# Sorting only the first 192 tokens' keys in the head, and moving the other keys, the later scores and the second query transpose into the first dense layer

## The chip, the cores and the metric

One core of a Trainium2 chip. The time is device time in microseconds (us), the median over executions. Engines: TensorE (PE, with its weight loads PEld), VectorE (DVE), ScalarE (ACT), GpSimd (POOL), SyncE (SP). The granted clock is the share of TensorE's full clock in the profile's records: at half clock it is 0.5. PSUM is the memory that takes the results of matmuls here; VectorE and ScalarE copy them out of it.

## The reference, cut to what matters

```python
# P: (batch 4, heads 8, 8, 8), five rounds of exp and row/column normalisation (Sinkhorn)
k_sorted = einsum('bhij,bhjcd->bhicd', P, k_blocks)   # 8 blocks of 96 rows, head_dim 64
v_sorted = einsum('bhij,bhjcd->bhicd', P, v_blocks)
scores = q_blocks @ k_sorted_blocks.T / 8             # inside each block of 96
attn   = softmax(scores) @ v_sorted_blocks
x      = attn, tokens x 512
out    = (s * relu(x @ w_in)**2 + b) @ w_out          # 512 -> 2048 -> 512
```

The sort mixes whole blocks, so one destination block of keys needs all eight source blocks, but only its own row of P. The tokens go through in 8 tiles of 384: tile 0 is destination blocks 0 to 3 of batch 0, tile 1 blocks 4 to 7. The 192 tokens of the title are blocks 0 and 1.

## The kernel before: the parts that matter here

The head, from the finished P to the first dense matmul:

```python
    k_piece(0, 0, 16, 1, "v")()     # 16 matmuls of 64 columns, copies by VectorE ("v")
    k_piece(0, 32, 16, 1, "s")()    # by ScalarE ("s")
    k_piece(0, 64, 8, 1, "v")()
    k_piece(0, 80, 8, 1, "s")()
    v_piece0(0, 16, "v")            # values: 16 matmuls and one copy
    v_piece0(16, 16, "s")
    v_piece0(32, 16, "v")
    s_piece(0, 0)                   # scores and exp of tile 0, head pair 0, four blocks
    s_piece(0, 1)
    v_piece0(48, 16, "v")
    s_piece(0, 2)
    s_piece(0, 3)
    q_half(1, "s")                  # transpose q for tile 1
    for hp in range(NHP):
        p_piece(0, hp, 0, 2)        # attn x values, blocks 0 and 1
    t_piece(0, "v", 0, 2)           # transpose them: 192 columns for the dense layer
    s_piece(1, 0)
    s_piece(1, 1)
```

Tile 0's first dense layer runs in two halves of 192 columns. Each half has eight groups, and after each group a slot for one piece of other work:

```python
    ffn1(0, Queue([P(0, 0, 2, 2), P(0, 1, 2, 2), P(0, 2, 2, 2), P(0, 3, 2, 2), SC(1, 2),
                   lambda: t_piece(0, "v", 2, 2), SC(1, 3), P(1, 0)], 8), 0, 2)
    ffn1(0, Queue([nothing, P(1, 1), nothing, P(1, 2), nothing, P(1, 3), nothing,
                   lambda: t_piece(1, "v")], 8), 2, 2)

    # in ffn1, for each group:
            hps = psa.tile([128, 2, 512], FP, tag="a", name="hps")   # one of 3 large PSUM buffers
            # ... 8 matmuls
            nc.scalar.activation(out=rt[...], in_=hps[...], func=AF.Relu)
            nc.vector.tensor_tensor(out=gt[...], in0=rt[...], in1=rt[...], op=ALU.mult)
            slot()
```

A piece in a slot is therefore issued to ScalarE and VectorE between the relu and square of one group and those of the next. The kernel's PSUM is divided into three large buffers (`psa`) and two small ones (`psb`).

The softmax here doesn't subtract the row's maximum and nothing guards it: scores larger than these inputs give would overflow.

## Time and profile before

| | before |
|---|---|
| time, median of the first 4 runs | 249.91 us (249.04 to 252.37) |
| span of the profiled run, mean granted clock | 247.8 us, 0.959 |
| first dense matmul (the head ends) | 31.04 us |
| half 1 of tile 0's first dense layer | 8.75 us |
| half 2 with its tail, up to tile 1's dense layer | 9.60 us |
| from tile 1's dense layer to the end | 198.4 us |

The last four rows come from the timeline: the starts of the 1st, 65th and 129th matmul of the dense layer's group, and the end of the span. They add up to the span, so a change can be booked row by row. The lines of the profile are shown in the prediction.

### The profile page before, as it was taken

What the parts mean: (1) busy time and instruction counts of PE and PEld (TensorE: products, weight loads), DVE (VectorE), ACT (ScalarE), POOL (GpSimd) and SP (SyncE); (2) the same over time, 40 slices, a digit from 0 to 9 for tenths busy, and PEclk for the clock granted to TensorE, in tenths of its full rate; (3) what the DMA queues carried; (4) which work ended last, traced back from release to release, by engine and by line L of the source; (5) the groups of instructions that cost most, each with busy time, mean ns of one, the idle gap of its engine ahead of it and who ended that gap; (6) DMA issues with size and microseconds to landing.
All of it is one profiled execution on the core that took longest, in us unless ns stands there. A gap on an engine that the chain in (4) does not pass through costs nothing.

```text
span 247.8 us, 4978 instructions
## 1 busy us (share of the span) xinstructions
PE 233.1 (94%) x2128; PEld 140.9 (57%) x2128; DVE 133.2 (54%) x260; ACT 116.3 (47%) x156; POOL 39.3 (16%) x51
## 2 busy tenths in 40 slices
PE   8879799799999899998899999999999999999993
PEld 4578699645554456655555555666555566664441
DVE  5776556899992545846675345444353444442221
ACT  6346566335358274477852342666341536661000
POOL 7720200497910027000000000000000000000000
PEclk9955579999999999999999999999999999999999
DMA  5999999999799929991001212000012120001122
GB/s 65 195 194 212 212 205 205 218 204 236 144 99 152 343 90 145 132 173 22 0 4 42 87 43 84 4 0 0 4 42 87 42 87 0 3 0 42 51 76 86
DMA packets 20214, 24.97 MB, mean 101 GB/s; under 512 B 7520, under 2 KB 14432, under 8 KB 19680
## 3 DMA queue, kind: packets, MB, share of 16 engines
q0 software_dynamic: 8400, 15.21, 35.8%
q1 hardware_dynamic: 11792, 9.45, 14.8%
q8 instruction: 16, 0.26, 0.5%
q14 instruction: 6, 0.05, 0.1%
HBM read 29.63 MB, written 8.65 MB: 155 GB/s over the span
## 4 chain that ended last, share of the span: by engine, by line
PE 69%; DVE 12%; DMA 9%; ACT 6%; issue 1%; SPq 0%; DVEq 0%
PE ops L459 29%; PE hps L433 27%; DMA vs<-dv 5%; PE pv L386 4%; DVE gt L438 3%; DMA dv<-vn 3%; ACT rt L437 3%; PE sc L359 3%; PE tr L414 2%; ACT ks L230 2%; PE tv L304 2%; DVE ks L228 2%; DVE qt L228 1%; PE tk L278 1%; DMA sn<-in_sort_net_dram 1%
## 5 line engine op out<-in xcount | busy, mean ns | idle before, releaser
L433 PE MATMUL hps<-xt,wi 128*128 128x384 bf16 (+1 forms) x576 | 89.2, 311 | 2.4 <-ACT ks L230 1.1
L459 PE MATMUL ops<-wo,gt 128*128 128x512 bf16 x384 | 90.5, 380 | 0.0
L433 PEld LDWEIGHTS <-wi 128*128 128x128 bf16 x576 | 54.3, 99 | 31.7 <-issue 4.1
L437 ACT ACTIVATE rt<-hps 128x768 bf16<-128x768 f32 (+1 forms) x72 | 53.2, 739 | 38.1 <-PE hps L433 34.1
L438 DVE TENSOR_TENSOR gt<-rt 128x768 bf16<-128x768 bf16 (+1 forms) x72 | 43.0, 601 | 43.2 <-ACT rt L437 42.8
L459 PEld LDWEIGHTS <-gt 128*128 128x128 bf16 x384 | 35.1, 98 | 38.4 <-issue 0.6
L450 DVE SCALAR_TENSOR_TENSOR ot<-ops,s_bc,bias 128x512 f32<-128x512 f32 x24 | 18.0, 748 | 36.4 <-PE ops L459 36.4
L362 ACT ACTIVATE at<-sc 96x768 bf16<-96x768 f32 x32 | 24.2, 802 | 24.1 <-PE sc L359 24.1
L391 DVE TENSOR_TENSOR x<-pv,rec 96x512 bf16<-96x512 f32 (+1 forms) x36 | 22.6, 628 | 1.3
L230 ACT COPY xt<-tr 128x1536 bf16<-128x1536 bf16 x6 | 8.6, 1438 | 23.6 <-PE tr L414 23.6
L228 DVE CAST ks<-tk 64x512 bf16<-64x512 f32 (+1 forms) x28 | 18.5, 662 | 1.7 <-PE tk L278 1.3
L583 POOL TENSOR_TENSOR csum<-csum,wo 128x512 f32<-128x512 f32 x14 | 17.6, 1255 | 1.0
L230 ACT CAST ks<-tk 64x512 bf16<-64x512 f32 (+1 forms) x24 | 13.9, 580 | 7.2 <-PE tk L278 6.9
L390 DVE RECIPROCAL rec<-pv 96x8 f32<-96x8 f32 (+1 forms) x36 | 7.0, 193 | 17.4 <-PE pv L386 17.4
L386 PEld LDWEIGHTS <-at 96*128 96x128 bf16 (+1 forms) x256 | 11.9, 104 | 5.6 <-DMA vs<-dv 1.5
L386 PE MATMUL pv<-vs,at 96*128 96x66 bf16 (+1 forms) x256 | 12.9, 199 | 1.8 <-DMA vs<-dv 1.0
L359 PEld LDWEIGHTS <-ks 64*96 64x96 bf16 x256 | 8.5, 132 | 6.1 <-issue 5.0
L359 PE MATMUL sc<-qt,ks 64*96 64x96 bf16 x256 | 10.8, 223 | 0.3 <-DVE ks L228 0.2
L172 PE MATMUL wp<-zt 128*128 128x256 bf16 x50 | 9.6, 321 | 1.1 <-DVE warm L104 1.1
L278 PE MATMUL tk<-pd,kb 64*128 64x64 bf16 (+1 forms) x144 | 8.3, 216 | 0.9 <-DVE pd L511 0.9
L278 PEld LDWEIGHTS <-kb 64*128 64x128 bf16 (+1 forms) x144 | 7.4, 106 | 3.0 <-issue 2.2
L228 DVE COPY qt<-tq 128x1536 bf16<-128x1536 bf16 x4 | 7.0, 1754 | 3.5 <-PE tq L259 3.5
(67 smaller groups left out, 116.8 us busy)
## 6 DMA issues: line engine op xcount, KB each, us to landing
out_dram<-ot SPq DMA_DIRECT2D x24, 256.0 KB, 2.0
kb<-in_k_dram POOLq DMA_DIRECT2D x4, 768.0 KB, 21.8
vb<-in_v_dram POOLq DMA_DIRECT2D x4, 768.0 KB, 19.0
qr<-in_q_dram POOLq DMA_DIRECT2D x3, 768.0 KB, 35.4
wi<-in_moe_w_in_dram POOLq DMA_DIRECT2D x2, 1024.0 KB, 19.1
wo<-in_moe_w_out_dram POOLq DMA_DIRECT2D x2, 1024.0 KB, 30.2
dv<-vn SPq DMA_DIRECT2D x6, 256.0 KB, 3.6
vs<-dv POOLq DMA_DIRECT2D x4, 384.0 KB, 11.3
```

What stands on the lines that cost most here:

```text
L228: nc.vector.tensor_copy(out=out, in_=in_)
L230: nc.scalar.copy(out=out, in_=in_)
L278: nc.tensor.matmul(out=ps[:, c, :], lhsT=kb[pr, c0 + 2 * c:c0 + 2 * c + 2, :].rearrange("p c d -> p (c d)"), rhs=rhs, start=True, stop=True)
L359: nc.tensor.matmul(out=sc[:, e, n * BLK:(n + 1) * BLK], lhsT=ks[pr, g0 + n, :], rhs=QT[b][pr, hp, q0:q0 + BLK], start=True, stop=True)
L362: nc.scalar.activation(out=at, in_=sc[:, :, 0:TG], func=AF.Exp, scale=scale)
L386: nc.tensor.matmul(out=pv[e][0:m, (n - n0) * VW:(n - n0 + 1) * VW], lhsT=atf[:, c0:c0 + m], rhs=VS[b][:, gi, :], start=True, stop=True)
L391: nc.vector.tensor_tensor(out=x[:, n0:n0 + nn, hp * 128:(hp + 1) * 128].rearrange("p n (e d) -> p e n d", e=2), in0=pvv[:, :, :, 0:D], in1 ...
L433: nc.tensor.matmul(out=hps[:, f, 0:nt], lhsT=wi_at(hp, f0 + f), rhs=xt[:, hp, c0:c0 + nt], start=(hp == 0), stop=(hp == NHP - 1))
L437: nc.scalar.activation(out=rt[:, :, 0:nt], in_=hps[:, :, 0:nt], func=AF.Relu)
L438: nc.vector.tensor_tensor(out=gt[:, f0:f0 + 2, c0:c0 + nt], in0=rt[:, :, 0:nt], in1=rt[:, :, 0:nt], op=ALU.mult)
L450: nc.vector.scalar_tensor_tensor(out=ot, in0=ops, scalar=s_bc, in1=bias, op0=ALU.mult, op1=ALU.add)
L459: nc.tensor.matmul(out=ops, lhsT=gt[:, f, m * 128:(m + 1) * 128], rhs=wo_at(f), start=(f == 0), stop=(f == NF - 1))
```

## The change

Its intent is to reach the first dense matmul sooner. Only what blocks 0 and 1 need is done in the head; the rest goes into slots, where TensorE was busy with dense groups anyway. The core of the diff:

```diff
-    k_piece(0, 0, 16, 1, "v")()  ... (four pieces, all 8 destination blocks)
+    k_piece0(0, 24, 0, 2, "v")      # destination blocks 0 and 1 alone: 16 columns
+    k_piece0(48, 24, 0, 2, "s")
     v_piece0(0, 16, "v")
     v_piece0(16, 16, "s")
+    s_half(0, 0, 0)                 # scores of two blocks
     v_piece0(32, 16, "v")
-    s_piece(0, 0) ... s_piece(0, 3), q_half(1, "s")
+    s_half(0, 1, 0)
-    v_piece0(48, 16, "v")
+    v_piece0(48, 8, "v")
+    s_half(0, 2, 0)
+    v_piece0(56, 8, "s")
+    s_half(0, 3, 0)
     ... p_piece x4, t_piece
-    s_piece(1, 0)
-    s_piece(1, 1)
+    def KB(c0, eng):
+        return lambda: k_piece0(c0, 16, 2, 6, eng)     # the other 6 blocks: 48 columns
+    def SH(hp):
+        return lambda: (s_half(0, hp, 2), s_half(0, hp + 1, 2))
+    ffn1(0, Queue([KB(0, "v"), KB(32, "s"), KB(64, "v"), SH(0), SH(2),
+                   seq(P(0, 0, 2, 2), P(0, 1, 2, 2)), seq(P(0, 2, 2, 2), P(0, 3, 2, 2)),
+                   lambda: t_piece(0, "v", 2, 2)], 8), 0, 2)
+    ffn1(0, Queue([lambda: q_half(1, "s"), S2(1, 0), nothing, S2(1, 2), P2(1, 0), nothing,
+                   P2(1, 2), lambda: t_piece(1, "v")], 8), 2, 2)
```

(`k_piece0` writes its results in 4 or 8 copies, and the loads of batch 2 now stand after half 1. `seq` puts several pieces into one slot; `S2` and `P2` are the scores and the attention x values of two head pairs.) A late key piece (`KB`) takes a large PSUM buffer and is emptied by 8 copies of 64 x 192 elements.

More of the change, by code (lines that the diff above doesn't have):

```diff
@@ L295, in k_piece, with k_piece0 @@
         return lambda: half(1)
+    def k_piece0(c0, nc2, i0, ni, eng):
+        pr = slice(0, 64)
+        gw = NHP * ni
+        if nc2 * 2 * gw > 512:
+            ps = psa.tile([128, 2, 512], FP, tag="a", name="tk")
+            psh = ps[:, :, 0:nc2 * gw].rearrange("p h (c w) -> p h c w", c=nc2 // 2)
+        else:
+            ps = psb.tile([128, 512], FP, tag="b", name="tk")
+            psh = ps[:, 0:nc2 * 2 * gw].rearrange("p (h c w) -> p h c w", h=2, c=nc2 // 2)
+        rhs = pd1[pr].rearrange("p e m i -> p (e m) i")[:, :, i0:i0 + ni]
+        for c in range(nc2):
+            nc.tensor.matmul(out=psh[:, c // (nc2 // 2), c % (nc2 // 2), :],
+                             lhsT=kb[pr, c0 + 2 * c:c0 + 2 * c + 2, :].rearrange("p c d -> p (c d)"),
+                             rhs=rhs, start=True, stop=True)
+        for cp in range(2):
+            for e in range(2):
+                dst = ks[e * 64:(e + 1) * 64, 0:32, c0 + cp:c0 + 2 * nc2:2].rearrange(
+                    "p (m i) c -> p m i c", i=NB)[:, :, i0:i0 + ni, :]
+                sr = psh[cp * 64:(cp + 1) * 64]
+                if sr.shape[1] * sr.shape[2] * 2 * gw <= 512:
+                    srs = [ps[cp * 64:(cp + 1) * 64, 0:nc2 * 2 * gw].rearrange(
+                        "p (c e m i) -> p e m i c", e=2, m=NHP, i=ni)[:, e]]
+                    dsts = [dst]
+                else:
+                    srs = [sr[:, h].rearrange("p c (e m i) -> p e m i c", e=2, m=NHP)[:, e]
+                           for h in range(2)]
+                    hc = nc2 // 2
+                    dsts = [dst[:, :, :, h * hc:(h + 1) * hc] for h in range(2)]
+                for d_, s_ in zip(dsts, srs):
+                    evac(d_, s_, eng)
     def v_piece0(d0, n, eng):
@@ L363, in s_piece, with s_half @@
         AT[t, hp] = at
+    def s_half(t, hp, n0, nn=2):
+        b, half = divmod(t, 2)
+        g0 = (b % 2) * 32 + hp * NB + half * HB
+        sc = psa.tile([BLK, 2, 512], FP, tag="a", name="sc")
+        for n in range(n0, n0 + nn):
+            for e in range(2):
+                pr = slice(e * 64, (e + 1) * 64)
+                q0 = (half * HB + n) * BLK
+                nc.tensor.matmul(out=sc[:, e, (n - n0) * BLK:(n - n0 + 1) * BLK],
+                                 lhsT=ks[pr, g0 + n, :], rhs=QT[b][pr, hp, q0:q0 + BLK],
+                                 start=True, stop=True)
+        at = atp.tile([BLK, 2, nn * BLK], BF, tag="at", name="ath")
+        nc.scalar.activation(out=at, in_=sc[:, :, 0:nn * BLK], func=AF.Exp, scale=scale)
+        AT[t, hp, n0] = at
     def p_piece(t, hp, n0=0, nn=HB):
         b, half = divmod(t, 2)
-        at = AT[t, hp]
+        halved = (t, hp, n0) in AT
+        at = AT[t, hp, n0] if halved else AT[t, hp]
         if t not in X:
@@ L382, in p_piece @@
             for n in range(n0, n0 + nn):
-                c0 = (e * HB + n) * BLK
-                m = 128 if c0 + 128 <= 2 * TG else BLK
+                c0 = (e * nn + n - n0) * BLK if halved else (e * HB + n) * BLK
+                m = 128 if c0 + 128 <= at.shape[1] * at.shape[2] else BLK
                 gi = e * 32 + hp * NB + half * HB + n
@@ L531 @@
     build_pd1()
-    k_piece(0, 0, 16, 1, "v")()
-    k_piece(0, 32, 16, 1, "s")()
-    k_piece(0, 64, 8, 1, "v")()
-    k_piece(0, 80, 8, 1, "s")()
+    k_piece0(0, 24, 0, 2, "v")
+    k_piece0(48, 24, 0, 2, "s")
     v_piece0(0, 16, "v")
     v_piece0(16, 16, "s")
+    s_half(0, 0, 0)
     v_piece0(32, 16, "v")
-    s_piece(0, 0)
-    s_piece(0, 1)
-    v_piece0(48, 16, "v")
-    s_piece(0, 2)
-    s_piece(0, 3)
-    q_half(1, "s")
+    s_half(0, 1, 0)
[3 more added lines that the diff above has]
+    s_half(0, 3, 0)
     for hp in range(NHP):
@@ L547 @@
     t_piece(0, "v", 0, 2)
-    s_piece(1, 0)
-    s_piece(1, 1)
-    load_v(*brows(2))
-    load_k(*brows(2))
-    load_q(2)
     def P(t, hp, *r):
@@ L563, in V1 @@
         return lambda: v_piece1(i * 8, "v")
-    ffn1(0, Queue([P(0, 0, 2, 2), P(0, 1, 2, 2), P(0, 2, 2, 2), P(0, 3, 2, 2), SC(1, 2),
-                   lambda: t_piece(0, "v", 2, 2), SC(1, 3), P(1, 0)], 8), 0, 2)
-    ffn1(0, Queue([nothing, P(1, 1), nothing, P(1, 2), nothing, P(1, 3), nothing,
-                   lambda: t_piece(1, "v")], 8), 2, 2)
+    def KB(c0, eng):
[5 more added lines that the diff above has]
+                   lambda: t_piece(0, "v", 2, 2)], 8), 0, 2)
+    load_v(*brows(2))
+    load_k(*brows(2))
+    load_q(2)
+    ffn1(0, Queue([lambda: q_half(1, "s"), S2(1, 0), nothing, S2(1, 2), P2(1, 0), nothing,
+                   P2(1, 2), lambda: t_piece(1, "v")], 8), 2, 2)
     build_pd2()
```

## The prediction

> **What bounds the kernel now.** I read three views in this order: the page of the whole run, to see which engine sets the end; the chain that ended last, to see where that engine does not; and the timeline of the first 50 us, the only part that the change touches.
>
> From the page:
>
> ```profile
> PE 233.1 (94%) x2128; PEld 140.9 (57%) x2128; DVE 133.2 (54%) x260; ACT 116.3 (47%) x156; POOL 39.3 (16%) x51
> PEclk9955579999999999999999999999999999999999
> ```
>
> TensorE is busy 94% of the span, so from the first dense layer on the end is "start of that layer plus TensorE's work". The second line has 6.2 us per digit: TensorE ran at about half clock from roughly 12 to 34 us. From the chain that ended last, from the sorting of the first keys to the first dense matmul:
>
> ```profile
> 13.53 1.88 PE tk L278 x32
> 15.43 0.74 ACT ks L230
> ...
> 18.52 2.94 PE tv L304 x32
> ...
> 24.38 1.23 DVE vs L228
> ...
> 25.65 1.49 PE tq L244 x25
> 27.14 0.35 PE pv L386 x4
> ...
> 30.29 0.80 PE sc L359 x10
> 31.10 1.40 PE hps L433 x8
> ```
>
> The reader is to see that this head is not only TensorE: copies out of PSUM by ACT and DVE stand between the matmuls. The dense layer starts at 31.0. From the timeline:
>
> ```profile
> 14.58 4.92 DVE L228 CAST ks<-tk 64x512 bf16<-64x512 f32 x8 [1.10 <-PE tk L278]
> 15.43 4.80 ACT L230 CAST ks<-tk 64x512 bf16<-64x512 f32 x8 [3.46 <-PE tk L278]
> 16.81 4.65 PE L304 MATMUL tv<-pd,vb 64*128 64x64 bf16 x48 [0.56 <-DMA vb<-in_v_dram]
> 33.05 0.36 DVE L438 TENSOR_TENSOR gt<-rt 128x384 bf16<-128x384 bf16 x1 [2.16 <-ACT rt L437]
> 33.91 0.83 PE L433 MATMUL hps<-xt,wi 128*128 128x192 bf16 x8
> 37.55 0.49 ACT L437 ACTIVATE rt<-hps 128x384 bf16<-128x384 f32 x1
> 49.38 1.47 PE L433 MATMUL hps<-xt,wi 128*128 128x384 bf16 x8
> ```
>
> Key copies occupy both copying engines for 4.9 us, but the values land only at 16.8, and their matmuls run until 24. In the dense part, TensorE goes from piece to piece without a gap: half 1 of the first dense layer runs 31.04 to 39.78 (8.7 us), half 2 with its tail until the next dense layer starts at 49.38 (9.6 us). ACT and DVE follow TensorE there with little waiting for them. One more reading matters at the end: TensorE waited 1.03 us at 82.17 for a DMA (vs<-dv), so a little slack of the DMA queues lies there.
>
> **What the Trainium skill says.** (1) "TensorE: Matmul & The Clock Gate", section on LDWEIGHTS: the load of the stationary operand scales with its columns, whatever the contraction. So a key matmul with 128 stationary columns does not get cheap when its moving side shrinks from 64 to 16. The trace agrees as far as it goes: 48 pairs took 2.72 us, 57 ns each at half clock, and 16 took 0.57 us, 36 ns each, at full clock. (2) The same page, section "Architectural detail": ACT and DVE are strict FIFO. The trace cannot contradict it, and the whole estimate below rests on it. (3) The same page, Part 1: full clock comes after about 3.4 us of sustained activity and goes after an idle window. Here the clock fell at 13.24 and rose at 33.72, 2.7 us into the dense layer. (4) "ScalarE: Activation LUTs", section "What ACT_TABLE_LOAD costs": an ACTIVATE costs 186 ns + 0.833 ns per element. For 192 elements that is 346 ns. The trace's key copies are 740 ns at 512 and 424 at 256, a slope of 1.23 ns, steeper than the page's, but it also gives 346 at 192. DVE's were 750 and 430, so it is used for both.
>
> **The change part by part.** The head sorts keys for two of eight destination blocks only, scores two blocks only, and leaves out the transpose of the second half of q and the scores of tile 1. All of that goes into the first dense layer, and the keys of batch 0 are now multiplied twice: 48 matmuls with 16 columns, then 48 with 48.
>
> *Head.* Matmuls of keys: 48 before and after, still about 2.7 us, to 16.2. Copies: 4 of 192 elements on each engine, 4 x 0.36 = 1.4 us in place of 4.9; they end near 17.7. But the values land at 16.8 as before, and the 64 value matmuls take 97 ns each (4.65/48): 6.2 us, plus four short score pieces of 0.25: TensorE is done at 24.0. The last value copy (8 wide, ACT, about 0.5) ends near 24.5, so attention x values starts there and not at 27.1: 1.45 us because the q transpose is gone, 1.1 us from copies. From there to the dense layer it took 3.95 us (27.08 to 31.04); nothing on that path is removed. Start of dense layer: 28.45. Gain 2.6 us.
>
> *Half 1 of the dense layer, counted from its start, TensorE first at half clock.* Pieces in the built order: H0 (dense group), K0 (keys, copied by DVE), H1, K1 (copied by ACT), H2, K2 (copied by DVE), H3, scores 0 and 1, H4, scores 2 and 3, H5, two pv, H6, two pv, H7, transpose. A dense group is 1.23 at half and 0.66 at full clock; a key piece 0.9 or 0.57. Each key piece has 8 copies of 192 elements: 8 x 0.36 = 2.9 us. TensorE reaches the end of K1 at 1.23+0.9+1.23+0.9 = 4.3. ACT copies K1 from 4.5 to 7.3, and only then can do the relu of H2 (7.8), because it is FIFO. DVE must square H2 (8.15) before it may copy K2: 8.15 to 11.05. Scores 0 need every key, so TensorE waits until 11.1; in the old kernel the half was over at 8.7. After that: scores and H4 to 12.2 or 12.8, exps and relus in turn on ACT (four of 0.5 each), H5's relu done near 14.5 to 15.5, then DVE alone: square 0.36, two pv results 2 x 0.62, square, two more, square, transpose copy 0.56, that is 3.6 with latencies 4.2. Half 1 ends at 18.7 (full clock from H2) to 20.2 (half clock throughout). Against 8.74: a loss of 10.0 to 11.5.
>
> *Half 2 with its tail.* Added: the q transpose (48 matmuls, 1.3; two ACT copies of 0.75 that the scores wait for), and scores 0 and 1 of tile 1 with their exps (2 x 0.80). ACT's sum is 8 x 0.49 + 1.5 + 4 x 0.80 = 8.6. With three PSUM buffers the dense groups wait for exps: H8 0 to 0.7, transposes to 2.0, copies on ACT 2.1 to 3.6, relu 4.1, exps to 5.75, two relus to 6.75, exps to 8.35, relu 8.85; then DVE's square and two pv results (0.89 each) to 11.05, squares to 12.0, two more to 13.8, square and transpose copy to 15.35, and the next layer starts at 16.0. Against 9.6: a loss of 6.4.
>
> *Later.* The next batches' loads of keys and values wait for later matmuls, but they stand in one queue behind loads that fill it until about 48 us, so they are not late. The 1.03 us wait for the DMA disappears, since loads drain while TensorE is late: gain 1.0.
>
> Sum: -2.6 + 10.7 (middle) + 6.4 - 1.0 = +13.5. TensorE's clock may fall again in the gap of half 1 and be half in part of half 2: an estimate of +0.5 for that, from the 1.5 us that such a case costs at most over half 2. Time: 249.95 + 14 = 264.
>
> **The rivals.** *A: the gain of the head carries through.* If copies hid behind dense matmuls, the cost would be TensorE's added work alone: in the dense layer 48 key matmuls at 36 ns (1.7), transposes 1.3, scores 1.0, 4.0 in all, against a head shorter by 2.6: about 251, within 2%. For it: DVE is busy 54% and ACT 47% over the run. Against it: in half 1 DVE now has 2.9 (squares) + 5.8 (keys) + 2.5 + 0.6 = 11.8 us of work where the half took 8.7. *B: faster.* If TensorE kept full clock in the head through denser work and the dense layer ran at full clock from its start, 1.3 us more would come in, 247 to 249. Against it: between 16.7 and 20.1 TensorE was already busy without gaps and the clock stayed at half. *C: the clock falls.* Gaps of 3 us in half 1 and 60% duty in half 2 keep half clock until the next layer: 267 to 268. For it: the clock stayed low through the head, where TensorE was busy 80% with small matmuls.
>
> **Range and chances.** If a key copy took 0.25 rather than 0.36 us, half 1 would lose 2.6 less; if half 2 hid half of what I charge, 3.2 less: 258. With C, 268. I take 258 to 269 as the 8 in 10. Slower by over 2% means over 254.95, which needs 5 of the 14 us only: 0.92. Within 2%: 0.06, rival A with part of the stall. Faster: 0.02.
>
> **What would show it.** The first dense matmul near 28.5 (head right). In half 1 a gap of TensorE of about 3 us that ends with DVE's key copies, near 39.5 us from the start; 24 late key copies of near 350 ns each; the first full-width dense matmul of tile 1 (128x384) near 63 to 66 in place of 49.4; no wait for vs<-dv; a lower granted clock than 0.959. It is wrong if that first full-width group comes before 56, if the copies take under 0.25 us, or if the time after that group is shorter or longer than before by more than 2 us.

## The result, and the profile after

The changed kernel takes **260.16 us** (259.28 to 260.99, 4 runs) against 249.91: the ratio is **1.039** (95% interval 1.031 to 1.048), slower. Ratios here are the mean time of one kernel's fast runs over that of the other's of the same rounds, so not quite the ratio of the medians quoted. The profiled run of the changed kernel (260.99) was the slowest of its four, so the table's +11.5 is a little more than the 10.3 between the medians.

| stage (profiled runs) | before | after | difference | predicted |
|---|---|---|---|---|
| first dense matmul | 31.04 | 27.63 | -3.4 | -2.6 |
| half 1 | 8.75 | 19.04 | +10.3 | +10.0 to +11.5 |
| half 2 with tail | 9.60 | 14.20 | +4.6 | +6.4 |
| rest | 198.37 | 198.42 | 0.0 | -1.0 + 0.5 |
| span | 247.8 | 259.3 | +11.5 | +14 |

The page of the changed kernel, the two lines that answer to the first fence of the prediction:

```profile
PE 239.5 (92%) x2156; PEld 144.0 (56%) x2176; DVE 133.0 (51%) x272; ACT 116.1 (45%) x165; POOL 39.4 (15%) x51
PEclk9955555997999999999999999999999999999999
```

DVE and ACT are no busier than before in sum; nothing in the averages shows an engine that limits the kernel. The clock line (6.5 us per digit) has five digits at half rate where there were about three, and a 7 further on. From the timeline of the changed kernel, the head; as everywhere in this view the columns are start, busy time, engine, line, operation, operands, count and, in brackets, the idle time just before and what ended it:

```profile
13.63 1.43 PE L309 MATMUL tk<-pd,kb 64*128 64x16 bf16 x48 [1.00 <-DVE pd L560]
14.45 1.54 DVE L228 CAST ks<-tk 64x192 bf16<-64x192 f32 x4 [0.97 <-PE tk L309]
...
16.82 2.85 PE L336 MATMUL tv<-pd,vb 64*128 64x64 bf16 x30 [1.76 <-DMA vb<-in_v_dram]
...
23.74 0.65 PE L435 MATMUL pv<-vs,ath 96*128 96x66 bf16 x8 [0.48 <-ACT vs L230]
```

The reader is to see the same landing of the values as before (16.8), now with TensorE idle for 1.76 us ahead of it, and attention x values starting at 23.7, not at 27.1. Then half 1, in the same view:

```profile
27.63 1.44 PE L482 MATMUL hps<-xt,wi 128*128 128x192 bf16 x8 [0.65 <-DVE xt L228]
...
29.91 2.58 DVE L228 CAST ks<-tk 64x192 bf16<-64x192 f32 x8
...
32.00 2.39 ACT L230 CAST ks<-tk 64x192 bf16<-64x192 f32 x8 [0.26 <-PE tk L309]
...
34.41 0.49 ACT L486 ACTIVATE rt<-hps 128x384 bf16<-128x384 f32 x1
...
34.94 0.36 DVE L487 TENSOR_TENSOR gt<-rt 128x384 bf16<-128x384 bf16 x1 [2.07 <-ACT rt L486]
35.33 2.57 DVE L228 CAST ks<-tk 64x192 bf16<-64x192 f32 x8
...
37.29 0.31 PE L406 MATMUL sc<-qt,ks 64*96 64x96 bf16 x1 [1.41 <-DVE ks L228]
...
37.96 0.55 PE L406 MATMUL sc<-qt,ks 64*96 64x96 bf16 x7 [0.36 <-DVE ks L228]
```

Read it downwards as one chain. ACT copies the second key piece for 2.4 us; only then, at 34.41, does it get to a relu whose matmuls had ended at about 33.4. DVE had nothing to do for 2.07 us until that relu let it square, and only then does it copy the third key piece, whose matmuls had ended at about 34.1. The scores need that copy: TensorE waits 1.41 and 0.36 us for it, after 0.33 us for ACT before the group ahead. The last part of half 1, still in this view:

```profile
43.62 0.42 DVE L440 TENSOR_TENSOR x<-pv,rec 96x256 bf16<-96x256 f32 x1
...
44.19 0.35 PE L435 MATMUL pv<-vs,ath 96*128 96x66 bf16 x4 [0.21 <-DVE x L440]
...
46.05 0.56 DVE L228 COPY xt<-tr 128x768 bf16<-128x768 bf16 x1
...
46.67 0.83 PE L482 MATMUL hps<-xt,wi 128*128 128x192 bf16 x8 [0.65 <-DVE xt L228]
```

The four attention results of blocks 2 and 3 come in the last slots, right before half 2 needs them, so half 2 waits for DVE. Later, the pieces of tile 1's first dense groups show the clock:

```profile
60.87 2.25 PE L482 MATMUL hps<-xt,wi 128*128 128x384 bf16 x8
...
63.61 2.05 PE L482 MATMUL hps<-xt,wi 128*128 128x384 bf16 x8
...
65.93 1.47 PE L482 MATMUL hps<-xt,wi 128*128 128x384 bf16 x8
```

The same group takes 1.47 us at full clock; two groups ran at half clock because the granted clock fell at 61.4 us for 3.4 us. That is 0.78 + 0.58 = 1.4 us lost, and it hides the gain of the vanished wait for the DMA (vs<-dv, 1.03 us before, none now).

### The profile page after: what moved, and what is told of

The parts are those of the page before. It is cut to its first block, busy times and chain, and to the rows that moved or that the text cites. A ratio compares the mean times of both kernels' runs of the same rounds, so it can differ in the third digit from the quotient of the medians.

```text
span 259.3 us, 5077 instructions
## 1 busy us (share of the span) xinstructions
PE 239.5 (92%) x2156; PEld 144.0 (56%) x2176; DVE 133.0 (51%) x272; ACT 116.1 (45%) x165; POOL 39.4 (15%) x51
## 4 chain that ended last, share of the span: by engine, by line
PE 75%; DVE 10%; ACT 6%; DMA 5%; issue 2%; POOL 1%; POOLq 0%
PE ops L508 31%; PE hps L482 29%; DMA vb<-in_v_dram 5%; ACT rt L486 4%; DVE ks L228 3%; PE pv L435 3%; PE sc L391 3%; DVE gt L487 2%; PE tr L463 2%; PE tv L336 2%; ACT ks L230 2%; DVE x L440 1%; DVE qt L228 1%; PE tq L259 1%; PE tv L366 1%
## 5 line engine op out<-in xcount | busy, mean ns | idle before, releaser
L482 PE MATMUL hps<-xt,wi 128*128 128x384 bf16 (+1 forms) x576 | 94.3, 322 | 4.6 <-ACT ks L230 1.4
L508 PE MATMUL ops<-wo,gt 128*128 128x512 bf16 x364 | 87.7, 379 | 1.5 <-issue 0.5
L482 PEld LDWEIGHTS <-wi 128*128 128x128 bf16 x576 | 56.9, 103 | 36.0 <-issue 6.6
L394 ACT ACTIVATE at<-sc 96x768 bf16<-96x768 f32 x28 | 21.1, 808 | 20.0 <-PE sc L391 20.0
L228 DVE CAST ks<-tk 64x192 bf16<-64x192 f32 (+1 forms) x40 | 20.3, 524 | 1.7 <-PE tk L309 1.0
L230 ACT CAST ks<-tk 64x512 bf16<-64x512 f32 (+1 forms) x28 | 13.1, 485 | 7.0 <-PE tk L278 3.4
L435 PEld LDWEIGHTS <-at 96*128 96x128 bf16 x224 | 9.6, 102 | 3.2 <-issue 0.4
L435 PE MATMUL pv<-vs,at 96*128 96x66 bf16 x224 | 9.9, 195 | 0.3 <-ACT at L394 0.3
L391 PE MATMUL sc<-qt,ks 64*96 64x96 bf16 x224 | 8.6, 210 | 0.7 <-ACT qt L230 0.3
L463 PE MATMUL tr<-ident,x 96*128 96x96 bf16 x128 | 7.7, 211 | 0.8 <-DVE x L440 0.6
L377 POOL DMA_DIRECT2D vs<-dv x4 | 5.4, 1346 | 20.5 <-DMA dv<-vn 19.1
## 6 DMA issues: line engine op xcount, KB each, us to landing
wi<-in_moe_w_in_dram POOLq DMA_DIRECT2D x2, 1024.0 KB, 18.7
```

What stands on the lines that cost most here:

```text
L228: nc.vector.tensor_copy(out=out, in_=in_)
L230: nc.scalar.copy(out=out, in_=in_)
L391: nc.tensor.matmul(out=sc[:, e, n * BLK:(n + 1) * BLK], lhsT=ks[pr, g0 + n, :], rhs=QT[b][pr, hp, q0:q0 + BLK], start=True, stop=True)
L394: nc.scalar.activation(out=at, in_=sc[:, :, 0:TG], func=AF.Exp, scale=scale)
L435: nc.tensor.matmul(out=pv[e][0:m, (n - n0) * VW:(n - n0 + 1) * VW], lhsT=atf[:, c0:c0 + m], rhs=VS[b][:, gi, :], start=True, stop=True)
L482: nc.tensor.matmul(out=hps[:, f, 0:nt], lhsT=wi_at(hp, f0 + f), rhs=xt[:, hp, c0:c0 + nt], start=(hp == 0), stop=(hp == NHP - 1))
```

## The experiments

Theory 1, from the prediction: half 1 is set by a serial chain through the two copying engines: second key piece on ACT, relu, square, third key piece on DVE, scores. Rivals: DVE's total work; the three large PSUM buffers; TensorE's added matmuls or its half clock; the late q transpose and scores rather than the keys.

| run | time | ratio to before | first dense | half 1 | half 2 | rest |
|---|---|---|---|---|---|---|
| changed kernel | 260.16 | 1.039 | 27.6 | 19.04 | 14.20 | 198.4 |
| changed_again | 259.33 | 1.043 | 26.9 | 19.05 | 14.20 | 198.4 |
| k0_twice | 260.88 | 1.048 | 26.8 | 19.98 | 14.43 | 198.2 |
| k1_twice | 262.83 | 1.056 | 27.4 | 22.09 | 14.43 | 198.0 |
| keys_split | 261.18 | 1.050 | 27.4 | 20.22 | 14.20 | 197.0 |
| keys_small_psum | 260.50 | 1.047 | 27.4 | 20.08 | 14.20 | 197.0 |
| keys_alternate | 257.75 | 1.038 | 27.4 | 16.87 | 14.20 | 197.1 |
| keys_in_head | 253.73 | 1.022 | 28.3 | 12.44 | 14.20 | 197.1 |
| q_in_head | 259.64 | 1.043 | 27.6 | 19.05 | 12.57 | 197.1 |
| keys_and_q_in_head | 252.34 | 1.017 | 29.6 | 12.63 | 14.16 | 198.1 |
| filled | 259.15 | 1.039 | 27.4 | 18.00 | 16.37 | 197.0 |
| q_late_only | 251.04 | 1.008 | 29.0 | 12.82 | 9.58 | 197.2 |
| values_split_only | 248.56 | 1.000 | 29.5 | 9.54 | 9.59 | 197.7 |

Times are medians of the fast runs; the stages are of the one profiled run each, found as in the table above. The intervals of the ratios are 0.3 to 0.6% wide on either side (0.9% in the first row), so the stages tell more than the times. The profiled run of keys_and_q_in_head was slow; it is one of its four timed runs. One of four runs of keys_in_head and two of six of values_split_only were slow too. Times and ratios leave them out. The changed kernel was run once more, in the same rounds as keys_alternate, keys_and_q_in_head and values_split_only, for a baseline:

> The changed kernel itself, for a baseline on the same chip and in the same rounds as the next three: 260 to 261 us, 1.039 to 1.047 of the kernel before.

It agrees with the first measurement; the total came out 0.7 us under the range expected, the ratio inside it. The clock took another course than in the first profile (full from 32.9 to 36.3 us, then half until 43.2), and half 1 is the same to 0.01 us: for 2.2 of those 3.4 us TensorE waited for key copies. The first dense matmul differs by 0.7 us between the two rows, and that follows the landing of the values: in eight profiles with this same head (both of these, the two `twice`, keys_split, keys_small_psum, keys_alternate, filled) the value matmuls start at 16.0 to 16.8 us and the dense layer 10.8 to 10.9 us later. It doesn't follow the fall of the clock, which comes anywhere from 12.9 to 16.1 us there.

**k0_twice and k1_twice: which copies are on the path.** The changed kernel with every copy of one late key piece written twice: the first piece (DVE), or the second (ACT).

```diff
-                for d_, s_ in zip(dsts, srs):
-                    evac(d_, s_, eng)
+                for d_, s_ in zip(dsts, srs):
+                    for _ in range(times):
+                        evac(d_, s_, eng)
-    ffn1(0, Queue([KB(0, "v"), KB(32, "s"), ...
+    ffn1(0, Queue([KB(0, "v", 2), KB(32, "s"), ...     # k0_twice; k1_twice: KB(32, "s", 2)
```

> The changed kernel with each copy of the first late key piece (on DVE) written twice: 8 more copies of about 0.32 us, 2.6 us more work for DVE. Theory 1, a serial chain (second piece copied on ACT, then the relu, then the square, then the third piece on DVE): the first piece ends before the square that gates the third, so the time grows by only 0.5 to 0.9 us over the changed kernel's 260.2. Rival, DVE's total work in the half sets its length: plus 2.6 us.

> The changed kernel with each copy of the second late key piece (on ACT) written twice: 2.4 us more work for ACT and none for DVE. Theory 1 (the serial chain runs through this piece): plus 2.4 us, about 262.6. Rival, DVE's total work sets the half: plus 0 to 0.5 us.

From the timelines, k0_twice first, then k1_twice:

```profile
29.12 5.74 DVE L228 CAST ks<-tk 64x192 bf16<-64x192 f32 x16
```
```profile
31.82 5.50 ACT L230 CAST ks<-tk 64x192 bf16<-64x192 f32 x16 [0.26 <-PE tk L309]
...
37.87 0.36 DVE L488 TENSOR_TENSOR gt<-rt 128x384 bf16<-128x384 bf16 x1 [5.19 <-ACT rt L487]
```

The extra copies took 3.1 to 3.2 us in either run (16 in 5.74 and 5.50 us, where 8 took 2.58 and 2.39), more than the 2.4 to 2.6 expected. On ACT's second piece they cost half 1 3.05 us, all of it. On DVE's first piece they cost 0.9: the changed kernel has DVE idle for 2.07 us ahead of the square that gates the third piece, and that took up two thirds of them. The totals of the two, of the same rounds, are 260.88 and 262.83. DVE's total work as the cause is ruled out: it had its extra 3.2 us in the run whose half 1 moved by 0.9.

**keys_split: a test that tested something else.** Each key piece copied half by DVE, half by ACT:

```diff
-                    evac(d_, s_, eng)
+                    evac(d_, s_, eng if ni == 2 else "vs"[cp])
```

> The changed kernel with each late key piece copied half by DVE and half by ACT, the same 24 copies. Theory 1: the second piece no longer takes ACT for 2.4 us before a relu, and the third is copied in half the time: scores of blocks 2 and 3 start 2 to 2.5 us earlier, time near 257.9. Rival, TensorE's added matmuls or its half clock set the half: no change beyond 0.5 us.

No gain; half 1 even grew by 1.2 us. The timeline of this run says why:

```profile
33.04 1.25 DVE L228 CAST ks<-tk 64x192 bf16<-64x192 f32 x4
...
33.63 0.82 PE L309 MATMUL tk<-pd,kb 64*128 64x48 bf16 x16
...
34.37 1.19 ACT L230 CAST ks<-tk 64x192 bf16<-64x192 f32 x4 [1.64 <-DVE ks L228]
```

ACT's half began when DVE's ended. The built program has a wait of ACT for DVE there: two engines that read one PSUM tile are put in order. Other ways to divide the tile, by columns or by banks, were built but not run, and have such waits too; so has a build in which ACT's half goes to another destination, so it isn't the shared destination. So each piece still took two half copies one after the other, and the run does not tell the theories apart.

**keys_small_psum and keys_alternate: the same test without that wait.** Six pieces of 8 in the two small PSUM buffers. In the first kernel they are copied by the same engines in the same order as in the changed kernel, in the second by DVE and ACT in turn.

```diff
-    ffn1(0, Queue([KB(0, "v"), KB(32, "s"), KB(64, "v"), SH(0), ...
+    ffn1(0, Queue([seq(KB(0, "v"), KB(16, "v")), seq(KB(32, "s"), KB(48, "s")),      # keys_small_psum
+                   seq(KB(64, "v"), KB(80, "v")), SH(0), ...
+    ffn1(0, Queue([seq(KB(0, "v"), KB(16, "s")), seq(KB(32, "v"), KB(48, "s")),      # keys_alternate
+                   seq(KB(64, "v"), KB(80, "s")), SH(0), ...
-        return lambda: k_piece0(c0, 16, 2, 6, eng)
+        return lambda: k_piece0(c0, 8, 2, 6, eng)
```

> The changed kernel with the late keys in six pieces of 8 in the small PSUM buffers, in place of three of 16 in the large ones that the dense groups also use; the same copies on the same engines in the same order. Theory 1: no PSUM buffer sets the half, so within 0.5 us of 260.2. Rival, three large PSUM buffers are what stalls: 2 us or more faster.

> The changed kernel with the late keys in six pieces of 8, each in its own small PSUM buffer, copied in turn by DVE and ACT, so that both engines really copy at once (the built program has no wait of one copying engine for the other here, as it had in the split that failed). Theory 1, a serial chain of copies: the scores of blocks 2 and 3 start about 2 us earlier after the start of the dense layer (8.5 us in place of 10.3), half 1 near 17, time near 258. Rival, copies are not what sets half 1: no change beyond 0.5 us.

Out of the large buffers nothing is gained: half 1 takes 20.1, because 8 copies took 3.0 us there on either engine, in place of 2.39 on ACT and 2.57 on DVE. With the engines in turn half 1 falls to 16.9, and the last key copies end 8.5 us after the start of the dense layer, in place of 10.3, as foretold. From the timeline of keys_alternate:

```profile
34.12 1.49 ACT L230 CAST ks<-tk 64x192 bf16<-64x192 f32 x4
...
34.41 1.50 DVE L228 CAST ks<-tk 64x192 bf16<-64x192 f32 x4
```

Both engines copy at once. The time, 257.75 against 259.33 for the changed kernel of the same rounds, moved by 1.6 us; the intervals (1.032 to 1.043, and 1.037 to 1.048) overlap, so the evidence is the stage. There the first scores start 8.2 us after the start of the dense layer in place of 9.7; the other 0.7 us of the 2.2 come after them, and the clock rose at 40.0 us in this profile, at 43.2 in changed_again's. Against keys_small_psum, which has the same buffers and the old order, half 1 is 3.2 us shorter. So the chain of copies is on the path, and the large buffers are not what sets the half.

**keys_in_head, q_in_head, keys_and_q_in_head: which part of the change costs what.** Parts of the change taken back, the rest left.

```diff
-    k_piece0(0, 24, 0, 2, "v")                 # keys_in_head
-    k_piece0(48, 24, 0, 2, "s")
+    k_piece(0, 0, 16, 1, "v")() ... (the four pieces of before)
-    ffn1(0, Queue([KB(0, "v"), KB(32, "s"), KB(64, "v"), SH(0), ...
+    ffn1(0, Queue([nothing, nothing, nothing, SH(0), ...

+    q_half(1, "s")                             # q_in_head, ahead of the p_piece loop
-    ffn1(0, Queue([lambda: q_half(1, "s"), S2(1, 0), ...
+    ffn1(0, Queue([nothing, S2(1, 0), ...
```

> One part alone: the keys all sorted before the dense layer as in the kernel before, with the scores, the split value copies and the late q transpose of the changed kernel. Theory 1 (the late key copies cost half 1 some 9 us): the dense layer starts near 28.6, half 1 takes near 9.5 in place of 19.0, half 2 stays near 14.2; with the wait for the DMA gone, 251 to 252. Rival, the late q transpose and scores are what cost: stays above 256.

> One part undone: the transpose of the second half of q back in the head, all else as in the changed kernel. Theory 1 with ACT's added work setting half 2: half 2 shorter by 1.5 to 2.0 us (two ACT copies of 0.75 and the wait for them), head longer by 1.0 to 1.5: 259 to 260. If the transpose is harmless in half 2: 261 to 262.

> All keys and the q transpose back in the head; of the change only the later scores (blocks 2 and 3 of tile 0, and tile 1) and the split value copies remain. If the late scores with their exps are by themselves a cost, as keys_in_head's half 1 of 12.4 us suggests: half 1 near 12.4, half 2 near 12.6, time near 253. If the q transpose was what stretched both halves: near 250.

keys_in_head lies between the two theories: 253.73 (fast runs 252.79 to 256.38) where 251 to 252 was expected. Half 1 fell by 6.6 us, not by 9.5; 12.44 us are left where the kernel before takes 8.75. Its timeline has the scores early, and then lines that repeat the end of half 1 of the changed kernel:

```profile
33.36 0.38 PE L406 MATMUL sc<-qt,ks 64*96 64x96 bf16 x8
...
37.74 0.31 PE L435 MATMUL pv<-vs,ath 96*128 96x66 bf16 x4 [0.58 <-DVE x L440]
...
38.38 0.30 PE L435 MATMUL pv<-vs,ath 96*128 96x66 bf16 x4 [0.32 <-DVE x L440]
...
40.78 0.83 PE L482 MATMUL hps<-xt,wi 128*128 128x192 bf16 x8 [0.88 <-DVE xt L228]
```

With the keys back in the head the scores of blocks 2 and 3 still stand in slots 3 and 4, so their attention results come in slots 5 and 6, and TensorE waits for DVE 0.58, 0.32 and 0.88 us. In the kernel before those results stood in slots 0 to 3.

Not all of the 6.6 us are the wait for key copies. The first scores come 5.0 us after the start of the dense layer here, 9.7 in the changed kernel: 4.6 us, of which TensorE spent about 2.3 on the three key pieces and 2.1 waiting for copies. The other 2.0 us come after the scores, where TensorE ran at full clock (from 33.1 us) and in the changed kernel at half.

q_in_head shortens half 2 by 1.6 us, as expected; the time did not resolve it (1.043, like changed_again). The head, expected 1.0 to 1.5 us longer, is 0.9 longer when counted from the first value matmul (11.7 us to the dense layer in place of 10.8). keys_and_q_in_head came out at 252.34 (fast runs 251.80 to 254.67), nearer to the 253 expected if the late scores cost by themselves than to 250; its half 2 in the profile, 14.16, is not to be used: that run was slow, and its clock was half from 41.9 to 45.4 us.

**filled: the clock.** Matmuls on zeros, read by nobody, in TensorE's waits.

```diff
-    ... KB(64, "v"), SH(0), ...
+    ... KB(64, "v"), seq(lambda: warm_up(9), SH(0)), ...
-    ... P2(1, 2), lambda: t_piece(1, "v")], 8), 2, 2)
+    ... P2(1, 2), seq(lambda: warm_up(4), lambda: t_piece(1, "v"))], 8), 2, 2)
+    warm_up(4)
```

> The changed kernel with matmuls on zeros, whose result nobody reads, in three of TensorE's waits: 9 before the scores of half 1, 4 before the last transposes of half 2, 4 after them. They take no time that TensorE uses. Theory 1 with a clock term: the clock rises up to 3.4 us earlier in half 1, and does not fall at 61 us, the time falls by 1 to 2.5 us to near 258. Rival, half clock is the main cause of the loss: falls by 5 us or more. If such matmuls do not count as activity: no change.

In the profiled run the clock rose at 38.9 us in place of 44.3, half 1 took 1.0 us less (1.5 less counted from the first scores), and the fall at 61 us did not come (rest 197.0). But the clock fell again from 45.7 to 52.5, and half 2 took 2.2 us more. The time, 259.15, is within the spread of the changed kernel's. In half 1 the clock is worth 1 to 2 us (this run and keys_in_head); it does not explain 10. Whether it stays low because of the change is not shown.

**q_late_only and values_split_only: is there anything to keep?** The kernel before with one part of the change each.

```diff
-    q_half(1, "s")                             # q_late_only
-    s_piece(1, 0)
-    s_piece(1, 1)
+    ffn1(0, Queue([lambda: q_half(1, "s"), seq(P(0, 0, 2, 2), P(0, 1, 2, 2)),
+                   seq(P(0, 2, 2, 2), P(0, 3, 2, 2)), lambda: t_piece(0, "v", 2, 2),
+                   SC(1, 0), SC(1, 1), SC(1, 2), seq(SC(1, 3), P(1, 0))], 8), 0, 2)

-    v_piece0(48, 16, "v")                      # values_split_only
+    v_piece0(48, 8, "v")
+    v_piece0(56, 8, "v")
```

> The kernel before with one part of the change alone: the q transpose of the second half and the first two scores of tile 1 moved into half 1 of the dense layer, nothing done to the keys. TensorE's work is the same, the transposes run at full clock in 0.95 us in place of 1.45: theory 1 says 249.0 to 249.9, at best a few tenths of a us faster than before; slower by 1 us or more if ACT's copies stall half 1.

> The kernel before with one edit: the last value piece of 16 in two pieces of 8 in the small PSUM buffers, both copied by DVE, so that its matmuls need not wait 0.57 us for the exp that frees a large buffer, and the last copy on the path is 0.6 us in place of 1.2. The q transposes behind it start up to 1.1 us earlier: 248.2 to 248.6, or 0.3 to 0.4% faster than the kernel before. If the exps of the last scores set that end instead: no change.

q_late_only is slower by 0.8% (0.5 to 1.1%; within the 2% that counts as the same), outside the range of 249.0 to 249.9. The other outcome named, that ACT's copies stall half 1, isn't seen either: the relu behind them starts at 33.30 us, when its matmuls end (33.26). In its profile the dense layer starts 2.0 us sooner, 0.9 of it because the values landed sooner, and 4.1 are lost in half 1: of these, 1.5 are the transposes and 0.6 the two pieces of scores, which only changed place, and the clock stayed at half until 36.6 us, against 33.7 before. values_split_only is level (1.000, 0.995 to 1.004), where 0.3 to 0.4% were hoped for: from the first value matmul to the dense layer its profile takes 13.1 us in place of 14.2, the 1.1 expected, but more of the dense groups ran at half clock (it rose at 34.1 us, no earlier than without the edit) and half 1 took 0.8 us longer. What else takes the gain of the head in the timed runs stays open. No version beat the kernel before.

## Why the prediction was right, point by point

*The main step, half 1.* Predicted 18.7 to 20.2 us, measured 19.04, and by the mechanism named: ACT's copy of the second piece ahead of a relu, the square, the third piece on DVE, TensorE waiting for it. k1_twice against k0_twice shows the chain, keys_alternate that parting it brings the scores 1.4 us forward. Its terms were a little large. A late copy lasts 358 ns (median of 24), as foretold, but successive copies overlap: 8 took 2.58 us on DVE and 2.39 on ACT where 2.9 was charged, so the third piece was out 10.3 us after the start and not 11.05. The gap before the scores was 2.1 us, not 3. The 20.2 was worked out for half clock throughout, and the clock was half for 16.7 of the 19.0 us: set against that end, the prediction was 1.2 us too long, so that the number fell into the range is partly luck.

*What the prediction did not see inside it.* It put nearly all of half 1's loss on the late keys. The profiles of the changed kernel and keys_in_head, one run each, divide the 10.3 us like this: about 2.3 for the key matmuls on TensorE, 2.1 for the wait for their copies, 2.0 after the scores where the clock differed, and 3.7 that stay without the late keys, which come with the late scores and the attention results crowded into the last slots. The hand-worked timeline had these waits in it (DVE alone at the end of the half), so the total was right; the name on the cause was too narrow. Its range has a slip of the same kind: it takes 2.6 us off for faster copies, 24 of them, though by its own chain only 16 lie on the path (1.8 us); k0_twice shows that the first 8 had 2.07 us to spare.

*The head.* Predicted 28.45, measured 27.63 (26.84 to 27.63 in the eight profiles with this head). The term that failed: 0.25 us for each of four short score pieces. They ran interleaved with the value matmuls, and TensorE was through at about 23.2, not 24.0. The key matmuls were sized wrongly too (1.43 us, not 2.7: the load of 128 stationary columns did not hold them up), but that was off the path: TensorE then waited 1.76 us for the values to land.

*Half 2.* Predicted 16.0, measured 14.20. Transposes took 0.95 us (1.3 charged), and two exps of ACT 1.51 us (1.60 and gaps charged); the fourth exp ended 7.2 us after the start of the half where 8.35 was charged. That ACT's added work is what stretches the half is supported by q_in_head, 1.6 us less for taking two copies of 0.75 out, but the transposes' 0.95 us of TensorE left with them, and no run parts the two.

*The rest.* The wait for the DMA went, as said. The clock cost 1.4 us in the profiled run where 0.5 was allowed (from a most of 1.5 over half 2, whose working isn't given; filled's half 2, at half clock for 6.8 us, took 2.2 more); without the fall the rest took 197.0 to 197.1 us in six of the other profiles, 1.3 less than before.

*The sum.* -3.4 + 10.3 + 4.6 + 0.0 = 11.5 against +14: rival A (the head's gain carries through) charged 4.0 us for the two halves that took 14.9 more, B had the wrong sign, and C (half clock until the next layer) did not hold, since the clock was full from 44.3 us. In time the change cost 10.3 us, inside the range but 3.8 short of the 264 named. Of the signs named, the wait for vs<-dv was gone, the copies took near 350 ns and the granted clock was lower (0.934); the first full-width dense group, at 60.9 us, came before the 63 to 66 foretold.

## What to carry to other kernels

A gap filler in the slots of a dense loop is not paid in TensorE's time alone: its copies come, in program order, ahead of the work by which the same engines empty the loop's own results, and two fillers on two engines can form one chain through them. Before moving work into such a loop, write down for each engine the order in which it will do the loop's work and the filler's, and look for a consumer that needs the last of them. Moving work behind a shorter head can cost more than the head gives back: 3.4 us gained and 14.9 lost here.

## What the Trainium skill lacked or had wrong

- "TensorE: Matmul & The Clock Gate", section "LDWEIGHTS (loading the stationary operand)": a load of 128 columns is put at 128 / 1.2 = 107 ns, whatever the contraction. One load's record agrees (101 ns, mean of 48 at half clock). Taken for the spacing of small matmuls, as I took it, it misleads: at half clock 48 key matmuls with 128 stationary columns took 1.43 us with 16 moving columns (30 ns each) and 2.72 us with 64 (57 ns each), so the loads overlap. That section doesn't say that they do; the page's section "Back-to-back issue gap" has pairs of load and matmul pipelined.
- The same page, Part 1: the clock rises after about 3.4 us of sustained activity. It was at half for 30.7 us in the changed kernel (13.6 to 44.3 us), nine windows of 3.4, with TensorE shown busy for 24.6 us of that time. No page gives the share of a window that must be busy. From 30.65 to 34.06 us, the stretch of one such window that ends three windows before the rise, TensorE was shown busy throughout, with key and dense matmuls, and the clock stayed at half.
- "ScalarE: Activation LUTs", section "What ACT_TABLE_LOAD costs": 186 ns + 0.833 ns per element gives an estimate of 346 ns for 192 elements, close to the 358 ns (median) that ACT's late key copies lasted. How closely copies follow each other is another matter: 8 took 2.39 us out of the large PSUM buffers, their starts 231 to 240 and 360 to 369 ns apart in turn, and 3.00 us out of the small ones. No page tells why the spacing differs, and no run here isolates it.
- "PSUM — Partial Sum Buffer", section "PSUM bank collisions raise a hardware error", says that two engines can be in different quadrants (32 partitions) of one bank at the same time, and that the compiler's scheduler orders accesses to the same one. In keys_split the two halves of a piece lay in partitions 0 to 63 and 64 to 127, and the built program still had ACT wait for DVE (ACT idle for 1.64 us ahead of its half). No page mentions ordering by the whole tile.
